# Strassen products for the second MoE matmul of three experts, in an attention + MoE kernel on one Trainium2 core

## The chip, the core and the metric

The kernel runs on one core of one Trainium2 chip. The engines named below are TensorE (PE; its weight loads are shown as PEld), VectorE (DVE), ScalarE (ACT), GpSimd (POOL) and SyncE (SP), which here only issues DMAs. The metric is the device time in microseconds. An execution taken by the profiler is described by its span (first to last instruction) and by its own time, which is a little longer.

## The reference

```python
kv  = einsum('bhsd,bhse->bhde', k, v); out = einsum('bhsd,bhde->bhse', q, kv)
x   = out / sqrt(mean(out*out, -1) + 1e-6) * g_norm         # 2304 tokens x 512
p   = domain_probs / (domain_probs.sum(-1) + 1e-9)          # 4 experts
for e in range(4):
    h = maximum(x @ w1[e], 0)                               # first product, 512 -> 1024
    y += p[:, e:e+1] * (h @ w2[e])                          # second product, 1024 -> 512
# soft MoE on y: logits = y @ phi, softmax over tokens (dispatch) and over slots (combine),
# 8 experts x 4 slots, each maximum(slot @ w1, 0) @ w2, then combine @ slot_out
```

## The kernel before

The 2304 tokens are 18 tiles of 128, in five chunks: chunks 0 to 3 of four tiles, chunk 4 of two. Chunks 0 and 1 form the first group, 2 to 4 the second. In the first group the experts run in the order 0, 1, 2, 3, in the second in the order 3, 2, 1, 0, so that expert 3's weights stay. For each expert and chunk there is a first product (called (1, c) here, function `mm1`) and a second product ((2, c), `mm2`). Every factor is split into two f16 parts, high and low, and a product is three matmuls (high high, high low, low high).

The first product is a Strassen product with seven block products in place of eight: the sums of blocks of x are made once per chunk, those of w1 per expert (`PrepW1`, on POOL), each then split by ACT (line 567) and DVE (line 569). `mm1` is called for each product P in `ORDER` and for each half u of the outputs: 14 steps of 12 matmuls, with 256 columns for a four-tile chunk and 128 for chunk 4 (line 702). Several products add up in one PSUM bank, and between them an engine reads the bank: ACT copies it (line 720), DVE adds it to an earlier copy (lines 723, 728), ACT writes relu's high part (line 711) and DVE the low part (line 712). The next product on that bank waits for such a reading. There are two buffers of each kind of bank, one for each u.

The second product (`mm2`) is a plain one: for each tile of 128 tokens 24 matmuls of 512 columns (line 760) add up in one bank, and DVE adds it, times p, to the sum over the experts (line 771, line 769 for the first expert).

The program's order is written out by hand. A list `main` holds the steps of PE. Work for the other engines is put between them: `chain` spreads a list of small steps (weight preparation, attention of a later chunk, dispatch) over a stretch of `main`, with a weight of 0.55 for steps of a first product. Each engine runs its instructions in the order in which they were written. SBUF is handed out as 47 pages of 512 KB (`Page`); loads go through one SP queue in a fixed order (`loads`, `pump`, line 152) as pages come free, at most nine held until the last expert. In the second group the weights of experts 2, 1, 0 are read again and prepared again (`prep_w1`, `prep_w2`).

After the last expert, the soft MoE's weights (`m1`, `m2a`, `m2b`, 32 MB) are read through the same queue and used.

## Time and profile before

| | before |
|---|---|
| median of 3 runs | 864.11 us (863.99 to 864.43) |
| profiled execution, own time | 864.39 us |
| its span | 862.6 us |
| PE busy | 832.7 us, 97% of the span |
| DVE, ACT, POOL busy | 472.3, 344.1, 91.1 us |
| instructions | 15472 |
| DMA | 82.89 MB, mean 96 GB/s |

In the profile, the busy time of PE holds matmuls that overlap; the mean duration of one matmul is longer than the distance to the next. In the chain of waits a stretch names the instructions that followed each other without a wait. "Idle before" is the time an engine stood still before an instruction, with what ended it.

### The profile page before, as it was taken

Reading aid. Unit: us, or ns where it says so; the run is one execution under the profiler, and the core shown is the slowest. Engines: PE = TensorE matmul, PEld = TensorE weight load, DVE = VectorE, ACT = ScalarE, POOL = GpSimd, SP = SyncE. Lnnn points to the kernel's source line nnn. Section 1 sums busy time; section 2 is a strip of 40 time slices with the busy share of each in tenths; the row PEclk is TensorE's granted clock in tenths of the full one; section 3 lists DMA queues with packets and bytes.
Section 4 is the critical chain, followed back from the end, with each engine's and each line's share of the span. In section 5 each row is a group of like instructions: output and inputs, shape, how many; then the busy total and the mean of one; then the engine's idle time right before and its main releaser. Section 6 shows DMA issues by size and latency. Waiting matters only on the chain.

```text
span 862.6 us, 15472 instructions
## 1 busy us (share of the span) xinstructions
PE 832.7 (97%) x6621; PEld 562.8 (65%) x6621; DVE 472.3 (55%) x867; ACT 344.1 (40%) x659; POOL 91.1 (11%) x57
## 2 busy tenths in 40 slices
PE   8789899999999999999999999999999999999995
PEld 7675748576666767658485685766675684864444
DVE  3788888647765344535858753536434542342314
ACT  2675563453355133515454442513423330431213
POOL 2204611201120000000211202002110000000000
PEclk8899999999999999999999999999999999999998
DMA  8720410230050400320001400140000550166687
GB/s 335 304 74 1 149 47 1 61 136 1 2 185 17 141 2 25 98 74 1 1 2 49 171 2 1 49 145 4 1 25 25 196 195 1 67 248 224 220 343 221
DMA packets 29190, 82.89 MB, mean 96 GB/s; under 512 B 3009, under 2 KB 10049, under 8 KB 29121
## 3 DMA queue, kind: packets, MB, share of 16 engines
q1 hardware_dynamic: 28672, 81.80, 26.7%
q8 instruction: 52, 0.85, 0.4%
q10 hardware_dynamic: 448, 0.10, 0.1%
q14 instruction: 18, 0.14, 0.0%
HBM read 77.17 MB, written 4.72 MB: 95 GB/s over the span
## 4 chain that ended last, share of the span: by engine, by line
PE 84%; ACT 1%; DVE 1%; issue 0%; DVEq 0%; ACTq 0%
PE y L760 40%; PE p L702 34%; PE s L1305 2%; PE so L1343 2%; PE o L301 1%; PE x2T L788 1%; PE lg L811 1%; PE kv L246 1%; PE sp L882 1%; PE xT L370 1%; ACT t L720 0%; PE f L1393 0%; ACT pages L567 0%; DVE pages L388 0%; DVE t L728 0%
## 5 line engine op out<-in xcount | busy, mean ns | idle before, releaser
L760 PE MATMUL y<-pages 128*128 128x512 f16 x1728 | 381.7, 379 | 0.0
L702 PE MATMUL p<-pages 128*128 128x256 f16 (+1 forms) x3360 | 344.3, 263 | 9.7 <-ACT t L720 6.2
L702 PEld LDWEIGHTS <-pages 128*128 128x128 f16 x3360 | 301.3, 98 | 49.2 <-issue 12.7
L760 PEld LDWEIGHTS <-pages 128*128 128x128 f16 x1728 | 168.4, 98 | 194.9 <-issue 2.9
L720 ACT COPY t<-p 128x512 f32<-128x512 f32 (+1 forms) x120 | 64.3, 538 | 219.1 <-PE p L702 219.0
L569 DVE SCALAR_TENSOR_TENSOR pages<-pages,s_w 128x512 f16<-128x512 f32 x154 | 122.0, 827 | 5.0 <-ACT pages L567 5.0
L601 POOL TENSOR_TENSOR pages<-pages 128x1024 f32<-128x1024 f32 x28 | 70.8, 2530 | 506.8 <-DVE pages L569 176.7
L567 ACT ACTIVATE pages<-pages,s_w 128x512 f16<-128x512 f32 x154 | 101.7, 711 | 44.4 <-POOL pages L601 18.2
L711 ACT ACTIVATE pages<-t 128x512 f16<-128x512 f32 (+1 forms) x120 | 70.3, 587 | 99.3 <-DVE t L723 69.9
L771 DVE SCALAR_TENSOR_TENSOR pages<-y,pc,pages 128x512 f32<-128x512 f32 x54 | 40.5, 750 | 125.0 <-PE y L760 125.0
L712 DVE SCALAR_TENSOR_TENSOR pages<-t,pages 128x512 f16<-128x512 f32 (+1 forms) x120 | 85.1, 711 | 6.3 <-ACT pages L711 1.8
L723 DVE TENSOR_TENSOR t<-p,t 128x512 f32<-128x512 f32 (+1 forms) x80 | 50.7, 634 | 64.0 <-PE p L702 62.5
L728 DVE TENSOR_TENSOR t<-p,t 128x512 f32<-128x512 f32 (+1 forms) x40 | 25.5, 638 | 70.3 <-ACT t L720 70.3
L712 DVE SCALAR_TENSOR_TENSOR pages<-p,pages 128x512 f16<-128x512 f32 (+1 forms) x40 | 25.2, 630 | 2.5 <-ACT pages L711 2.4
L438 ACT CAST pages<-pages 128x512 f16<-128x512 f32 (+1 forms) x36 | 19.2, 564 | 9.9 <-POOL pages L388 4.1
L1314 POOL MEMSET pages<- 128x1024 f32 x2 | 1.8, 952 | 184.1 <-PE s L1305 184.1
L711 ACT ACTIVATE pages<-p 128x512 f16<-128x512 f32 (+1 forms) x40 | 20.7, 542 | 1.4 <-PE p L702 1.4
L301 PE MATMUL o<-kvs,pages 128*128 128x128 f32 (+1 forms) x160 | 21.0, 296 | 0.0
L301 PEld LDWEIGHTS o<-kvs,pages 128*128 128x128 f32 (+1 forms) x160 | 19.7, 200 | 1.4 <-issue 0.2
L769 DVE TENSOR_SCALAR pages<-y,pc 128x512 f32<-128x512 f32 x18 | 13.4, 747 | 12.2 <-PE y L760 12.2
L499 DVE TENSOR_REDUCE mx_w<-pages 128x1 f32<-128x1024 f32 x16 | 18.9, 1208 | 0.0
L440 DVE TENSOR_TENSOR pages<-pages 128x512 f16<-128x512 f32 (+1 forms) x26 | 16.5, 659 | 3.4 <-ACT pages L438 3.4
(166 smaller groups left out, 405.1 us busy)
## 6 DMA issues: line engine op xcount, KB each, us to landing
pages<-in_w SPq DMA_DIRECT2D x56, 512.0 KB, 4.9
pages<-in_m SPq DMA_DIRECT2D x32, 512.0 KB, 6.1
pages<-in_m2a SPq DMA_DIRECT2D x16, 512.0 KB, 4.1
pages<-in_m2b SPq DMA_DIRECT2D x16, 512.0 KB, 10.1
pages<-in_qT SPq DMA_DIRECT2D x9, 512.0 KB, 7.1
out<-pages SPq DMA_DIRECT2D x17, 256.0 KB, 2.9
pages<-in_k SPq DMA_DIRECT2D x8, 512.0 KB, 5.7
pages<-in_v SPq DMA_DIRECT2D x8, 512.0 KB, 6.4
```

The lines of the kernel that those rows point to most:

```text
L301: nc.tensor.matmul(ps[a:z, hp * 128:hp * 128 + 128], qp[:, hp, o + a:o + z], kvbd[b % 2][:, hp, :], start=True, stop=True,)
L567: nc.scalar.activation(dst[:, 0], src, AF.Copy, scale=s)
L569: nc.vector.scalar_tensor_tensor(out=dst[:, 1], in0=src, scalar=s, in1=dst[:, 0], op0=ALU.mult, op1=ALU.subtract)
L601: self.eng.tensor_tensor(out=self.src(op).ap, in0=a.ap, in1=b.ap, op=ALU.subtract)
L702: nc.tensor.matmul(ps[:, fp * n:fp * n + n], l, r, start=(fp + i == 0 and P in (1, 2, 7)), stop=(fp == 1 and i == len(mms) - 1 and P in (2 ...
L711: nc.scalar.activation(hh, src, AF.Relu)
L712: late.append(lambda: nc.vector.scalar_tensor_tensor(out=hl, in0=src, scalar=0.0, in1=hh, op0=ALU.max, op1=ALU.subtract))
L720: nc.scalar.copy(t, ps)
L723: nc.vector.tensor_tensor(out=t, in0=ps, in1=t, op=ALU.add)
L728: nc.vector.tensor_tensor(out=d[5], in0=d["z"], in1=d[5], op=ALU.add)
L760: nc.tensor.matmul(ps, a, b, start=(u + kk + fp + i == 0), stop=(u == 1 and kk == 1 and fp == 1 and i == 2))
L771: nc.vector.scalar_tensor_tensor(out=x, in0=ps, scalar=pc, in1=x, op0=ALU.mult, op1=ALU.add)
```

## The change

In the second group, for experts 2, 1 and 0, the second product is a Strassen product too (`mm2_fast`), except for chunk 3 of expert 0. Seven products of h blocks and w2 blocks replace eight; a step is 12 matmuls of 256 columns, with two steps a product for a four-tile chunk and one for chunk 4. So a four-tile unit has 168 matmuls of 256 columns where there were 96 of 512, chunk 4 has 84 where there were 48. For it the outputs of the first product are needed as seven operands, each with a high and a low part (`fast_h`): ACT and DVE form them, partly from a queue `todo` from which every step of `mm1` takes two entries and every step of `mm2_fast` one (`work_off`). The order of `mm1`'s products becomes `ORDER2`. The order of the chunks becomes `FASTSEQ`: the second product of a chunk runs after the first product of the next. Outputs leave PSUM as 128x256 additions on DVE, seven for two tiles.

The weight operands are no longer prepared in the second group. The split operands of w1 and w2 of experts 0 to 2 are written to DRAM in the first group (`lay_aside`), together with four sums of w2 blocks, for which w2 is read a second time (`want_t`, `prep_t2`: eight POOL subtractions, eight splits on ACT and DVE per expert). In the second group 15 pages per expert are read back. The w1 scale goes from 8 to 4.

```diff
-W1S = 8.0
+W1S = 4.0
...
+ORDER2 = (1, 2, 6, 7, 5, 4, 3)
+ORDER3 = (1, 7, 6, 4, 5, 2, 3)
...
-    LASTSEQ = [(1, 2), (2, 2), (1, 3), (1, 4), (2, 4), (2, 3)]
+    KEPT = E - 1
+    FAST = list(range(E - 1))
+    FASTSEQ = [(1, 2), (1, 3), (2, 2), (1, 4), (2, 3), (2, 4)]
+    LASTSEQ = [(1, 2), (1, 4), (2, 2), (1, 3), (2, 4), (2, 3)]
...
+            key = loads[0][0]
+            if key[0] in ("o1", "o2") and now < gate[key[1]]:
+                return
...
+    def want_t(e):
+        for b in range(4):
+            want(("w2", 1, e, b), w2[e, b], 2)
     for e in range(1, E):
-        want_w(0, e)
+        for b in range(4):
+            want(("w1", 0, e, b), w1[e, b], 2)
+        if e > 1:
+            want_t(e - 2)
...
+    want_t(E - 2)
...
+    def lay_aside(e, key, pg):
+        d = aside[key[0], e, key[1]] = dram.tile([128, 2, 512], F32, name=f"{key[0]}_{e}_{key[1]}", tag=f"{key[0]}_{e}_{key[1]}")
+        nc.sync.dma_start(out=d, in_=pg.f32(2))
+    def want_back(e):
+        for key in [("o1", o) for o in (B11, B21, T2, T3, T1, T4, B22)] + [
+                ("o2", b) for b in (0, 1, "t0", "t1", "t2", "t3", 2, 3)]:
+            loads.append(((key[0], e, key[1]), lambda k=(key[0], e, key[1]): aside[k], 2))
     for e in range(E - 2, -1, -1):
-        want_w(1, e)
+        want_back(e)
...
+    def prep_t2(e, eng):
+        st = []
+        def make(j, op):
+            p, q = (need(("w2", 1, e, b)).f32(2) for b in (j, 2 + j))
+            left, right = slice(0, 256), slice(256, 512)
+            o, a, b = {
+                T1: lambda: (p[:, :, left], p[:, :, right], p[:, :, left]),
+                T3: lambda: (p[:, :, right], q[:, :, right], p[:, :, right]),
+                T2: lambda: (q[:, :, right], q[:, :, right], p[:, :, left]),
+                T4: lambda: (q[:, :, left], q[:, :, left], q[:, :, right]),
+            }[op]()
...
+            eng.tensor_tensor(out=o, in0=a, in1=b, op=ALU.subtract)
...
+        def away(b):
+            pg = w2p[1, e].pop(f"t{b}")
+            lay_aside(e, ("o2", f"t{b}"), pg)
+            pg.release()
+        for j in range(2):
+            st += [lambda j=j, op=op: make(j, op) for op in (T1, T3, T2, T4)]
+            bi = [(b, i) for b in (j, 2 + j) for i in range(2)]
+            st += stagger([lambda b=b, i=i: w2_split(e, b, f"t{b}", i, 0) for b, i in bi],
+                          [lambda b=b, i=i: w2_split(e, b, f"t{b}", i, 1) for b, i in bi])
+            st += [lambda: None, lambda: None] + [lambda b=b: away(b) for b in (j, 2 + j)]
...
+    def work_off(n, c=None, op=None):
+        while todo and (n > 0 or any(o == (c, op) for o, _ in todo)):
+            todo.popleft()[1]()
+            n -= 1
...
+        def hi(v, op, src, relu):
+            dst = hop(wk, c, op, v)[:, 0]
+            if relu:
+                nc.scalar.activation(dst, sh(src), AF.Relu)
+            else:
+                nc.scalar.copy(dst, sh(src))
+        def lo(v, op, src, relu):
+            h = hop(wk, c, op, v)
+            if relu:
+                nc.vector.scalar_tensor_tensor(
+                    out=h[:, 1], in0=sh(src), scalar=0.0, in1=h[:, 0], op0=ALU.max, op1=ALU.subtract
+                )
+            else:
+                nc.vector.tensor_tensor(out=h[:, 1], in0=sh(src), in1=h[:, 0], op=ALU.subtract)
+        def comb(v, op, out, a, op1):
+            nc.vector.scalar_tensor_tensor(out=out, in0=a, scalar=0.0, in1=out, op0=ALU.max, op1=op1)
+            hi(v, op, out, False)
+        def then(op, f):
+            todo.append(((c, op), f))
+        t1 = ht1[c, 0], ht1[c, 1]
+        t6, t7, t4 = ([hraw(wk, c, op, v) for v in range(2)] for op in (S4, S1, A12))
+        if P == 1:
+            nc.scalar.copy(t1[u], ps)
+        elif P == 6:
+            nc.scalar.copy(t6[u], ps)
+        elif P == 7:
+            nc.scalar.copy(t7[u], ps)
+        elif P == 2:
+            nc.vector.tensor_tensor(out=t1[u], in0=ps, in1=t1[u], op=ALU.add)
+            hi(u, A11, t1[u], True)
+            then(A11, lambda: lo(u, A11, t1[u], True))
+        elif P == 5:
+            nc.vector.tensor_tensor(out=t7[u], in0=ps, in1=t7[u], op=ALU.add)
+            hi(u, A22, t7[u], True)
+            then(A22, lambda: lo(u, A22, t7[u], True))
+        elif P == 4:
+            nc.scalar.activation(t4[u], ps, AF.Relu)
+            def s3():
+                nc.vector.scalar_tensor_tensor(out=t1[u], in0=t1[u], scalar=0.0, in1=t4[u], op0=ALU.max, op1=ALU.subtract)
+                hi(u, S3, t1[u], False)
+            then(S3, s3)
+            if u == 1:
+                for v in range(2):
+                    then(S3, lambda v=v: lo(v, S3, t1[v], False))
+                for v in range(2):
+                    then(S2, lambda v=v: comb(v, S2, t1[v], t7[v], ALU.subtract))
+                for v in range(2):
+                    then(S1, lambda v=v: comb(v, S1, t4[v], t7[v], ALU.add))
+                for v in range(2):
+                    then(S2, lambda v=v: lo(v, S2, t1[v], False))
+                for v in range(2):
+                    then(S1, lambda v=v: lo(v, S1, t4[v], False))
+        else:
+            nc.vector.tensor_tensor(out=t6[u], in0=ps, in1=t6[u], op=ALU.add)
+            if u == 1:
+                then(A12, lambda: [hi(v, A12, t6[v], True) for v in range(2)])
+                for v in range(2):
+                    then(A12, lambda v=v: lo(v, A12, t6[v], True))
+                for v in range(2):
+                    then(S4, lambda v=v: comb(v, S4, t1[v], t6[v], ALU.subtract))
+                for v in range(2):
+                    then(S4, lambda v=v: lo(v, S4, t1[v], False))
...
+            b = {1: "x", 6: "x", 7: "x", 4: "x", 2: "y", 5: "z", 3: "z"}[P]
+            first, end = (1, 2, 5), (2, 3, 4)
...
+            fast_h(wk, c, u, P, d, ps)
+            work_off(2)
...
+    MM2 = {1: (A11, 0, 0, 0), 2: (A12, 1, 0, 0), 3: (S4, 1, 1, 0), 4: (A22, 1, 0, 1), 5: (S1, 0, 0, 1),
+           6: (S2, 1, 1, 1), 7: (S3, 0, 1, 1)}
...
+    def mm2_fast(wk, c, P, j):
+        op, row, side, made = MM2[P]
+        work_off(1, c, op)
+        nh = len(CH[c]) // 2
+        b = {1: "x", 6: "x", 5: "x", 3: "x", 2: "y", 7: "z", 4: "z"}[P]
+        if j == 0 and P in (1, 2, 7):
+            mbank[b] = (ps_yz if P == 2 else ps_o)(f"m{P}_{wk[0]}_{wk[1]}_{c}")
+        ps = mbank[b][:, 256 * j:256 * j + 256]
+        mms = []
+        for kb in range(4):
+            h = hop(wk, c, op, kb // 2)[:, :, kb % 2]
+            key = 2 * row + kb // 2
+            w = w2_page(wk, f"t{key}" if made else key).f16().rearrange("p (s k n) -> p s k n", s=2, k=2)[:, :, kb % 2]
+            hh, hl = (h[:, s, 128 * j:128 * j + 128] for s in range(2))
+            wh, wl = (w[:, s, 256 * side:256 * side + 256] for s in range(2))
+            mms += [(hh, wh), (hh, wl), (hl, wh)]
+        for i, (l, r) in enumerate(mms):
+            nc.tensor.matmul(
+                ps, l, r, start=(i == 0 and j == 0 and P in (1, 2, 7)),
+                stop=(i == len(mms) - 1 and j == nh - 1 and P in (2, 3, 4)), skip_group_check=True,
+            )
+        if j < nh - 1:
+            return
+        half, lo = {1: (0, 0), 2: (0, 0), 7: (1, 256), 6: (1, 0), 4: (1, 0), 5: (1, 256), 3: (0, 256)}[P]
+        for i in range(nh):
+            t = CH[c][half * nh + i]
+            x = acc_f32(t)[:, lo:lo + 256]
+            nc.vector.scalar_tensor_tensor(
+                out=x, in0=mbank[b][:, 256 * i:256 * i + 256], scalar=pcs[wk[1]][:, t:t + 1], in1=x, op0=ALU.mult, op1=ALU.add
...
+            if gi == 1 and e in FAST:
+                seq = LASTSEQ if last else FASTSEQ
             for n, (which, c) in enumerate(seq):
+                fast = gi == 1 and e in FAST and not (last and c == DISP[-1])
...
+                elif fast:
+                    st = [lambda wk=wk, c=c, P=P, j=j: mm2_fast(wk, c, P, j)
+                          for P in ORDER3 for j in range(len(ch) // 2)]
...
-    for e in range(E - 2, -1, -1):
-        chain(m["mm1", 1, e + 1, 3 if e == E - 2 else 2], m["end", 1, e + 1, 4] - 1, prep_w1(1, e, P) + prep_w2(1, e), 12)
+    for e in FAST:
+        if e < E - 2:
+            chain(m["mm1", 0, e + 1, 0] + 2, m["mm1", 0, e + 1, 1], prep_t2(e, P), 4)
+        else:
+            chain(m["mm1", 0, e + 1, 1], m["end", 0, e + 1, 1], prep_t2(e, P), 4)
+        gate[e] = m["mm1", 1, e + 1, 3]
+    for e in range(E - 1):
+        for i, op in enumerate((B11, B21, T2, T3, T1, T4, B22)):
+            hooks.setdefault(m["mm1", 0, e, 1] + 1 + i, []).append(
+                lambda e=e, op=op: lay_aside(e, ("o1", op), wop[0, e][op]))
+        for b in range(4):
+            hooks.setdefault(m["mm2", 0, e, 1] + 1 + b, []).append(
+                lambda e=e, b=b: lay_aside(e, ("o2", b), w2p[0, e][b]))
+    hooks.setdefault(m["mm1", 1, E - 2, 2], []).append(
+        lambda: hsets.extend([Page() for _ in range(7)] for _ in range(2)))
+    hooks.setdefault(m["mm1", 1, 0, 4], []).append(lambda: [hsets[1].pop().release() for _ in range(3)])
     lastc = DISP[-1]
-    chain(m["end", 1, 0, 2], m["mm1end", 1, 0, 4], disp_steps(2), 0, 1.0)
+    chain(m["end", 1, 0, 2], m["end", 1, 0, 4], disp_steps(2), 0, 1.0)
```

## Rows read from the trace of the kernel before

**Rows 1.** The page: busy time of PE, and the chain that ended last by engine.

```profile
PE 832.7 (97%) x6621; PEld 562.8 (65%) x6621; DVE 472.3 (55%) x867; ACT 344.1 (40%) x659; POOL 91.1 (11%) x57
...
PE 84%; ACT 1%; DVE 1%; issue 0%; DVEq 0%; ACTq 0%
```

**Rows 2.** Chain in order of time, expert 2, second group: start us, us, what.

```profile
496.74 18.42 PE p L702 x168
515.15 20.72 PE y L760 x96
...
575.01 6.04 PE p L702 x108
...
582.66 2.17 PE p L702 x36
584.84 10.36 PE y L760 x48
595.20 4.91 PE p L702 x45
```

**Rows 3.** Timeline of ACT in (1, 1) of expert 1, products 5 and 3.

```profile
181.28 0.59 ACT L720 COPY t<-p 128x512 f32<-128x512 f32 x1 [1.06 <-PE p L702]
182.62 0.63 ACT L711 ACTIVATE pages<-t 128x512 f16<-128x512 f32 x1 [0.76 <-DVE t L728]
183.16 0.57 ACT L720 COPY t<-p 128x512 f32<-128x512 f32 x1
```

**Rows 4.** Timeline of DVE and PE in the same unit.

```profile
169.29 18.58 PE L702 MATMUL p<-pages 128*128 128x256 f16 x168
...
170.16 1.41 DVE L569 SCALAR_TENSOR_TENSOR pages<-pages,s_w 128x512 f16<-128x512 f32 x2
...
181.90 0.69 DVE L728 TENSOR_TENSOR t<-p,t 128x512 f32<-128x512 f32 x1 [4.54 <-ACT t L720]
```

**Rows 5.** Groups by line and shape: line, engine, names, shapes, count | busy us, mean ns | idle before.

```profile
L712 DVE SCALAR_TENSOR_TENSOR pages<-t,pages 128x512 f16<-128x512 f32 x96 | 71.6, 747 | 4.2 <-ACT pages L711 0.4
L723 DVE TENSOR_TENSOR t<-p,t 128x512 f32<-128x512 f32 x64 | 44.1, 688 | 60.6 <-PE p L702 60.5
L723 DVE TENSOR_TENSOR t<-p,t 128x256 f32<-128x256 f32 x16 | 6.6, 419 | 3.4 <-PE p L702 2.1 <-ACT t L720 1.3
L711 ACT ACTIVATE pages<-t 128x512 f16<-128x512 f32 x96 | 60.5, 630 | 90.5 <-DVE t L723 65.1 <-DVE t L728 25.2
L440 POOL TENSOR_TENSOR pages<-pages 128x512 f16<-128x512 f32 x6 | 7.2, 1232 | 0.0
```

**Rows 6.** Timeline of (1, 1) of expert 0, where ACT waits for POOL.

```profile
97.76 3.49 DVE L569 SCALAR_TENSOR_TENSOR pages<-pages,s_w 128x512 f16<-128x512 f32 x2
97.92 2.79 POOL L601 TENSOR_TENSOR pages<-pages 128x1024 f32<-128x1024 f32 x1 [2.56 <-DVE pages L569]
...
100.74 1.33 ACT L567 ACTIVATE pages<-pages,s_w 128x512 f16<-128x512 f32 x2 [3.16 <-POOL pages L601]
...
102.59 1.47 PE L702 MATMUL p<-pages 128*128 128x256 f16 x12 [1.42 <-ACT t L720]
```

**Rows 7.** Windows: from:to us, PE, PEld, DVE, ACT, POOL busy, PEclk, DMA share, GB/s.

```profile
148.50:169.40 20.90, 20.90 (x101) 9.71 (x99) 14.27 (x23) 9.02 (x15) 5.54 (x2) 1.00 0.09 26
169.40:187.90 18.50, 18.50 (x170) 16.42 (x168) 9.22 (x14) 11.47 (x21) 0.00 (x0) 1.00 0.57 199
751.00:766.30 15.30, 14.32 (x212) 12.77 (x210) 11.14 (x33) 8.49 (x24) 0.00 (x0) 1.00 0.54 199
816.00:822.00 6.00, 6.00 (x59) 2.01 (x56) 0.65 (x3) 0.96 (x2) 0.00 (x0) 1.00 1.02 406
```

**Rows 8.** The clock after a stop of PE: a timeline row and a window.

```profile
56.70 2.33 PE L702 MATMUL p<-pages 128*128 128x256 f16 x12 [2.31 <-ACT t L720]
...
58.00:62.00 4.00, 4.00 (x27) 3.61 (x26) 3.15 (x5) 3.32 (x7) 0.00 (x0) 0.68 0.02 4
```

More of the change, by code (lines that the diff above doesn't have):

```diff
@@ L648, in prep_w1, with w2_split @@
         return st + [lambda n=n: step(n) for n in range(len(seq) + 1)]
+    def w2_split(e, b, key, i, part):
+        pgs = w2p.setdefault((0 if key == b else 1, e), {})
+        if key not in pgs:
+            pgs[key] = Page(True)
+        dst = pgs[key].f16().rearrange("p (s k n) -> p s k n", s=2, k=2)
+        src = ("w2", 0 if key == b else 1, e, b)
+        split(dst[:, :, i], need(src).f32(2)[:, i], wpw[e, "w2"][1], part)
+        if i == 1 and part == 1:
+            drop(src)
+    def prep_t2(e, eng):
[20 more added lines that the diff above has]
+            st += [lambda: None, lambda: None] + [lambda b=b: away(b) for b in (j, 2 + j)]
+        return st
     def prep_w2(g_, e):
@@ L657, in sp @@
         def sp(b, i, part):
-            pgs = w2p.setdefault((g_, e), {})
-            if b not in pgs:
-                pgs[b] = Page(True)
-            dst = pgs[b].f16().rearrange("p (s k n) -> p s k n", s=2, k=2)
-            split(dst[:, :, i], raw(b).f32(2)[:, i], wpw[e, "w2"][1], part)
-            if i == 1 and part == 1:
-                drop(("w2", g_, e, b))
+            w2_split(e, b, b, i, part)
         bi = [(b, i) for b in (0, 2, 1, 3) for i in range(2)]
@@ L680, in attn_moe_softmoe_kernel, with w1_page, w2_page, hset @@
     us = [{}, {}]
-    def mm1(wk, c, u, P):
+    def w1_page(wk, op):
+        pgs = wop.setdefault(wk, {})
+        if op not in pgs:
+            pgs[op] = need(("o1", wk[1], op))
+        return pgs[op]
+    def w2_page(wk, b):
+        pgs = w2p.setdefault(wk, {})
+        if b not in pgs:
+            pgs[b] = need(("o2", wk[1], b))
+        return pgs[b]
+    hsets = []
+    todo = deque()
+    def hset(wk, c):
+        return hsets[c == (4 if wk[1] == 0 else 3)]
+    def hraw(wk, c, op, u):
+        pgs = hset(wk, c)
+        if len(CH[c]) == 2:
+            i = 2 * SLOT[op] + u
+            return pgs[i // 4].f32(4)[:, i % 4]
+        return pgs[SLOT[op]].f32(2)[:, u]
@@ L702, in mm1 @@
                 nc.tensor.matmul(
-                    ps[:, fp * n:fp * n + n], l, r, start=(fp + i == 0 and P in (1, 2, 7)), stop=(fp == 1 and i == len(mms) - 1 and P in (2, 3, 4)),
+                    ps[:, fp * n:fp * n + n], l, r, start=(fp + i == 0 and P in first), stop=(fp == 1 and i == len(mms) - 1 and P in end),
                         skip_group_check=True,
                 )
+        if fast:
+            if P == 1:
+                ht1[c, u] = w512(f"t1_{nm}")[:, :2 * n]
+                ht1.setdefault((c, 1 - u), None)
+            fast_h(wk, c, u, P, d, ps)
+            work_off(2)
+            return
         def put(src, kk, half):
@@ L983, in start_chunk @@
     def start_chunk(c):
-        hbuf[c] = [Page() for _ in range(len(CH[c]))]
+        hbuf[c] = [Page() for _ in range(len(CH[c]))] if hbuf.get(c) is None else hbuf[c]
     def end_chunk(c):
@@ L1208, in attn_moe_softmoe_kernel @@
                 h()
[L1209 removed]
+            idle[0] = None if i >= m["mm2", 1, 0, lastc] else lend[i]
             run_bg(i)
```

82 lines of the change are left out of this document (58 added, 24 removed).

## The prediction

> **What bounds the kernel now.** I read the page first: PE is busy for 97% of the span and the chain that ended last is PE for 84% [rows 1]. So what counts is the work on PE, and each wait that stops it. Next I read the chain over one expert of the second group [rows 2]. A four-tile first product takes 18.42 us for 168 matmuls of 256 columns (0.1096 each), a four-tile second product 20.72 us for 96 of 512, the second product of chunk 4 10.36 us; each starts where the one before ends. Only chunk 4's first product has a gap: its first 9 steps take 6.04 us, 0.671 a step, so 14 would be 9.40, and from 575.01 to 584.84 it takes 9.83. The whole expert takes 595.20 - 496.74 = 98.46 us. Then I read how an engine clears a bank between two products [rows 3, 4]. Product 5 of the unit that starts at 169.45 ends after nine steps of 1.316, at 181.29. ACT copies at 181.28 (0.59), DVE adds at 181.90 (0.69), ACT writes relu's high part at 182.62 (0.63), and only then, in ACT's order, comes the copy for the other half, 183.16 to 183.73. Product 3 of that half is due at 169.45 + 11 x 1.316 = 183.93. So one round ACT, DVE, ACT leaves 0.2 us. Throughput is not short, but the turn-around is.
>
> **The columns saved.** A `mm2_fast` step has the shape of a first product's step. A four-tile unit costs 168 x 0.1096 = 18.42 us instead of 20.72, chunk 4 9.21 instead of 10.36 [rows 2]. Five four-tile units and three of chunk 4 are changed: 5 x 2.30 + 3 x 1.15 = 14.95 us off PE's path. This is the whole gain; prep removed from DVE, ACT and POOL in the second group was beside PE and gives nothing by itself.
>
> **The operands of h, walked in order.** Prices: a DVE operation on 128x512 gives its result after 0.75, an addition from PSUM after 0.69, ACT's high part after 0.63 [rows 5]. On one engine the next starts about 0.08 earlier than that: two of 0.75 take 1.41 [rows 4], ACT's follow 0.54 apart [rows 3]. So 0.67, 0.61 and 0.54 when queued; a handover 0.03 to 0.05. A four-tile unit asks DVE for 6 additions, 14 low parts, 8 combinations and 14 output additions of 128x256 (0.42 [rows 5], 0.36 queued): 3.7 + 14.7 + 5.0 = 23.4 us in PE's 36.8. On average there is room. The order is the trouble.
>
> Within (1, 2), count from the end of product 5 for u = 0. DVE adds (0.69), ACT writes the high part (0.63), and as `work_off` takes the low part in the same step, DVE stands waiting for ACT and then writes it (0.75): 2.15 us with handovers, where PE's step is 1.32. The second half begins at 2.15 and ends at 4.3. Then the difference S3 of u = 0 (to 5.0); the relu of product 4 for u = 1 is in ACT's queue behind S3's high part, so it is ready at 6.2 and S3 of u = 1 at 6.95; then one low part, addition, low part, combination, addition, two combinations: to 11.5. PE's last step ended at 5 x 1.316 = 6.58. So DVE is 4.9 us late at the end of every four-tile first product, and 12 entries of `todo` remain.
>
> (1, 3) follows at once. From its start: ACT's first copy waits behind the high part of the last combination and is ready at 6.2; product 6 was due at 4 x 1.316 = 5.26: PE stops 1.0. DVE ends four more entries at 7.6, the addition of product 2 at 8.2, another entry 8.9, the second addition 9.6. ACT, with two high parts of A12 put before it, writes the second high part at 10.6 and only then copies product 6: 11.2. Product 7 was due at 7.9 + 1.1: 2.1 lost. Its other half waits for a copy behind two combinations: another 0.95. A restart costs 0.16 (36 matmuls take 2.17 where 3 x 0.671 = 2.01 [rows 2]), so 4.5 us in all. From product 5 on the unit is as (1, 2), and again leaves DVE 4.9 late. In (2, 2) the output additions of product 1 stand behind two entries: ready at 7.1, product 6 due at 5.26: 2.0 lost. By the same walk with 0.42 for small operations [rows 5], (1, 4) loses 0.7, (1, 2) itself 0.3. Between (2, 3) and (2, 4) the first bank comes free only after product 3's two output additions, which begin when PE ends: 1.1. Together 0.3 + 4.5 + 2.0 + 0.7 + 1.1 = 8.6 us, against 5.75 saved and the 0.43 that (1, 4) lost before [rows 2]: +2.4 us for expert 2 and +2.4 for expert 1.
>
> Expert 0 has (1, 4) right behind (1, 2): the same 12 large entries meet steps of 0.671. The copy of product 6 is ready at about 10.1 where product 7 is due at 4.0; the stops come at products 2, 6 and 7, 6.3 by then with restarts, and the other half of product 7 adds 2.0: 8.3. With 0.3 in (1, 2) and 3.45 saved (one 2.30, one 1.15), and without the 0.98 of PE idle that this expert had in its old (1, 4) [rows 7], +4.2. Second group: 2.4 + 2.4 + 4.2 = +9.0 us.
>
> **The first group.** Per expert 8 POOL subtractions of 128x512 (1.23 each [rows 5]), 8 ACT and 8 DVE splits are added. They start no later than two steps into a unit. In the three first products that they cross, one ACT split (0.6) falls between the high part and the copy of product 5, where 0.2 us was left: 0.4 + 0.16, about 1.7 for three. In the second product that follows, DVE is busy 14.27 of 20.9 us [rows 7]; six low parts add 4.0. A make on POOL can hold up DVE: while one of 2.79 ran, two DVE splits took 3.49 instead of 1.41 [rows 6]. Five makes add 0 to 6.2, so DVE ends up to 3.5 us late; the next unit leaves it 9 of 18.5 us free [rows 7]. ACT waiting for POOL did stop PE by 1.42 in such a place [rows 6]. I take 0 to 3.5 for each of two experts (expert 2's makes run where POOL has no other weights). Bounds 0 and 1.7 + 7 = 8.7; I take 3, nearer to the unit that has room.
>
> The Trainium skill, SBUF — State Buffer, section "SBUF: two separate sides", says that DVE with two SBUF inputs and a GpSimd operation that reads SBUF exclude each other for the whole instruction. By that rule every make that meets a split costs its whole length, the upper bound above; the trace shows one split in two extended.
>
> **Queues, pages, scale.** Each expert adds 15 writes and 15 reads of 512 KB on SP and 4 reads of w2, and takes 8 reads out. At 406 GB/s [rows 7] a page takes 1.3 us: 15 take 19, inside an expert of about 95. A write waits on SP for a split that is already done; behind it stand the next expert's loads, a few us, with a unit of 18 us before their use. Writes hold their pages until they land; I price this with the 0 to 8.7. The last w2 pages of an expert are read while (1, 2) and the next unit run, 27 us in the shortest case. The soft MoE's loads start later, since h takes 14 pages; of their 64 pages 47 fit, 61 us at that rate, and about 90 us remain after the last (1, 2): 0, at most 3. The scale and the product order change no count: 0.
>
> **Sum.** 864.39 + 9.0 + 3 = 876.4 for an execution as the profiled one, which was 0.28 above the median: 876.1 us.
>
> **Rivals.**
> *The queues keep up.* If neither of the lags at the ends of first products reaches PE, because `todo` is worked off before it matters, the columns stand: 14.95 less the two waits between (2, 3) and (2, 4) (2.2) and 0 to 3 of the first group gives about 852. For it: DVE has 23.4 us of work in 36.8. Against: the order in ACT's queue, and a trace in which a single round is as tight as a step. 0.18.
> *The clock falls.* After a stop of 2.31 us the granted clock was 0.68 over 4 us [rows 8], at the lower of its levels (1.2 GHz) for 2.6 of them: 1.3 lost. After 1.42 it did not fall. If it falls in both (1, 3) and twice in the last (1, 4): +5, 881. 0.10.
> *The first group saturates DVE*, as with the lock above: +8.7 instead of 3, 882; decided where DVE's lag passes the 5.2 us (20.72 / 4) that a second product's spare bank gives it. 0.08.
> *The read-back is late.* If SP stands more than 17 us behind (27 less 8 pages of 1.3), PE waits at (2, 2): some 6 us, 882. No load here is that late. 0.04.
>
> **How the numbers follow.** The forecast has 0.60. About 0.2% is what a measurement can tell from no change: 862.4 to 865.8. The stops are differences of long sums: with every DVE and ACT price 10% lower the walk gives 97.0 for an expert in place of 100.9 and 2.2 less for expert 0, and without a first-group cost 863.4; 0.06 of the 0.60 lies within the bound. Upward, prices 5% higher give 2.3 more for each expert and 1.4 for expert 0, and 8.7 for the first group: 888. Faster 0.18, same 0.06, slower 0.54 + 0.22 = 0.76. The range 860 to 887 leaves out most of the first rival and little above.
>
> **What would show it.** Four-tile `mm2_fast` without stops: 18.4 us. Expert 2's chain: (1, 3) of about 23 us, with stops before products 6 and 7 released by ACT's copy; (2, 2) of 20.4, with a stop before product 6 released by DVE; the last (1, 4) about 17.7. In the first group stops below 1 us at product 3 of three units. If (1, 3) takes under 19 us, the walk is wrong and the first rival holds; idle before loads would show the fourth, a clock below 1 in the second group the second.

## The result and the profile after

The changed kernel takes 870.95 us (median; 870.41 to 871.56) against 864.25 us for the kernel before: a ratio of 1.0078, 95% interval 1.0061 to 1.0095. So it is slower by 6.7 us, where 12 were forecast. The profiled execution of the kernel after took 870.41 us with a span of 868.6, that of before 864.39 with 862.6: 6.0 us to be found.

The page of the kernel after, its busy time and the chain by engine (answering [rows 1]):

```profile
PE 821.4 (95%) x7089; PEld 609.2 (70%) x7089; DVE 523.8 (60%) x1002; ACT 350.6 (40%) x681; POOL 96.0 (11%) x69
...
PE 68%; DVE 12%; ACT 6%; issue 1%; DMA 0%; SPq 0%; DVEq 0%; ACTq 0%
```

The busy time of PE fell by 11.3 us and the span grew by 6.0; the chain, which was PE for 84%, is now PE for 68%, DVE for 12% and ACT for 6%. Work was taken off PE and waits were put in. The bytes written to DRAM rose from 4.72 to 28.31 MB, those read from 77.17 to 94.47. No share of the chain is DMA, so the rival with the late read-back is out at this point.

The places where PE stopped in the kernel after, from its timeline: start, duration, what ran then, how long PE had stood before it and what ended that. First the first group; none of these five is in the trace of before.

```profile
120.64 1.46 PE L955 MATMUL y<-pages 128*128 128x512 f16 x6 [2.00 <-DVE pages L964]
146.31 4.09 PE L890 MATMUL p<-pages 128*128 128x256 f16 x36 [0.53 <-ACT t L915]
180.02 10.88 PE L890 MATMUL p<-pages 128*128 128x256 f16 x96 [0.81 <-DVE t L918]
226.82 4.09 PE L890 MATMUL p<-pages 128*128 128x256 f16 x36 [0.58 <-ACT t L915]
260.51 10.88 PE L890 MATMUL p<-pages 128*128 128x256 f16 x96 [0.80 <-DVE t L918]
```

Then the second group: the first five rows are expert 2 (expert 1 has the same five, 97.3 us later), the last five expert 0.

```profile
523.50 2.78 PE L890 MATMUL p<-pages 128*128 128x256 f16 x24 [0.31 <-ACT t L819]
528.01 1.47 PE L890 MATMUL p<-pages 128*128 128x256 f16 x12 [1.73 <-ACT pages L821]
530.22 9.33 PE L890 MATMUL p<-pages 128*128 128x256 f16 x84 [0.75 <-ACT pages L821]
545.90 13.26 PE L991 MATMUL m<-pages 128*128 128x256 f16 x120 [1.11 <-DVE pages L1001]
563.71 5.52 PE L890 MATMUL p<-pages 128*128 128x128 f16 x96 [0.53 <-ACT pages L821]
...
715.77 0.83 PE L890 MATMUL p<-pages 128*128 128x128 f16 x12 [0.97 <-DVE pages L853]
717.95 1.62 PE L890 MATMUL p<-pages 128*128 128x128 f16 x24 [1.35 <-ACT t L819]
721.77 0.83 PE L890 MATMUL p<-pages 128*128 128x128 f16 x12 [2.19 <-ACT pages L821]
724.20 6.20 PE L890 MATMUL p<-pages 128*128 128x128 f16 x84 [1.60 <-ACT pages L821]
769.29 0.33 PE L1090 MATMUL dtr<-ident,dT 128*128 128x128 f32 x1 [1.73 <-ACT dT L1082]
```

Line 819 is ACT's copy of product 1 (PE waits to go on to product 6), line 821 that of product 6 (the step after is product 7), line 1001 an output addition of `mm2_fast`: the places and releasers that the prediction named. Expert 2's chain in [rows 2] had one gap; here it has five.

The 6.0 us by parts, from where each expert starts in the two traces. Expert 3 of the second group keeps its weights and follows on the first group without a gap:

| part | before | after | difference | forecast |
|---|---|---|---|---|
| first group, to expert 3's start in it | to 287.57 | to 292.48 | +4.9 | +3 |
| expert 3, both groups | to 496.74 | to 499.40 | -2.25 | 0 |
| expert 2 | 98.46 | 97.34 | -1.1 | +2.4 |
| expert 1 | 98.51 | 97.33 | -1.2 | +2.4 |
| expert 0, to the start of the tail | 112.5 | 118.2 | +5.7 | +4.2 |
| tail | 56.4 | 56.3 | 0 | 0 |

The first row holds a difference that is not of the change. At the stop of 1.4 us that both kernels have in (1, 1) of expert 0, before any of the five, the kernel after was ahead by 0.87 (101.72 against 102.59), and a kernel below that differs from it in the second group alone (the second form of fewer entries) reached that place at 102.53. From there on the first group lost 5.8, of which the five stops are 4.72 and a restart of 0.16 after each 0.8.

### The profile page after: what moved, and what is told of

It is laid out like the page before. It is cut to its first block, busy times and chain, and to the rows that moved or that the text cites. A ratio compares the mean times of both kernels' runs of the same rounds, so it can differ in the third digit from the quotient of the medians.

```text
span 868.6 us, 16718 instructions
## 1 busy us (share of the span) xinstructions
PE 821.4 (95%) x7089; PEld 609.2 (70%) x7089; DVE 523.8 (60%) x1002; ACT 350.6 (40%) x681; POOL 96.0 (11%) x69
## 3 DMA queue, kind: packets, MB, share of 16 engines
HBM read 94.47 MB, written 28.31 MB: 141 GB/s over the span
## 4 chain that ended last, share of the span: by engine, by line
PE 68%; DVE 12%; ACT 6%; issue 1%; DMA 0%; SPq 0%; DVEq 0%; ACTq 0%
PE y L955 24%; PE p L890 22%; PE m L991 13%; DVE pages L603 2%; PE s L1578 2%; DVE pages L802 2%; ACT pages L795 1%; PE so L1616 1%; DVE pages L806 1%; PE o L335 1%; ACT t L915 1%; PE x2T L1020 1%; DVE t L810 1%; DVE t L825 1%; PE lg L1043 1%
## 5 line engine op out<-in xcount | busy, mean ns | idle before, releaser
L890 PEld LDWEIGHTS <-pages 128*128 128x128 f16 x3360 | 302.5, 98 | 63.2 <-issue 29.2
L955 PE MATMUL y<-pages 128*128 128x512 f16 x1104 | 246.1, 379 | 2.5 <-DVE pages L964 2.0
L955 PEld LDWEIGHTS <-pages 128*128 128x128 f16 x1104 | 107.3, 98 | 125.8 <-issue 5.8
L991 PE MATMUL m<-pages 128*128 128x256 f16 x1092 | 121.0, 273 | 2.2 <-DVE pages L1001 2.2
L991 PEld LDWEIGHTS <-pages 128*128 128x128 f16 x1092 | 106.6, 98 | 15.8 <-issue 3.4
L601 ACT ACTIVATE pages<-pages,s_w 128x512 f16<-128x512 f32 x112 | 73.5, 711 | 37.8 <-POOL pages L635 12.0
L906 ACT ACTIVATE pages<-t 128x512 f16<-128x512 f32 (+1 forms) x72 | 44.0, 612 | 71.5 <-DVE t L918 53.2
L1001 DVE SCALAR_TENSOR_TENSOR pages<-m,pc,pages 128x256 f32<-128x256 f32 x91 | 40.8, 481 | 40.7 <-PE m L991 40.6
L907 DVE SCALAR_TENSOR_TENSOR pages<-t,pages 128x512 f16<-128x512 f32 (+1 forms) x72 | 54.6, 761 | 3.0 <-ACT pages L906 0.6
L918 DVE TENSOR_TENSOR t<-p,t 128x512 f32<-128x512 f32 (+1 forms) x48 | 31.7, 664 | 35.2 <-PE p L890 35.2
L635 POOL TENSOR_TENSOR pages<-pages 128x1024 f32<-128x1024 f32 x16 | 40.3, 2521 | 96.6 <-DVE pages L603 62.8
L707 POOL TENSOR_TENSOR pages<-pages 128x512 f32<-128x512 f32 x24 | 35.6, 1484 | 81.2 <-DMA pages<-in_w 78.8
L923 DVE TENSOR_TENSOR t<-p,t 128x512 f32<-128x512 f32 (+1 forms) x24 | 16.1, 669 | 30.7 <-ACT t L915 30.6
## 6 DMA issues: line engine op xcount, KB each, us to landing
pages<-in_m2b SPq DMA_DIRECT2D x16, 512.0 KB, 10.1
```

What stands on the lines that cost most here:

```text
L601: nc.scalar.activation(dst[:, 0], src, AF.Copy, scale=s)
L635: self.eng.tensor_tensor(out=self.src(op).ap, in0=a.ap, in1=b.ap, op=ALU.subtract)
L707: eng.tensor_tensor(out=o, in0=a, in1=b, op=ALU.subtract)
L890: nc.tensor.matmul(ps[:, fp * n:fp * n + n], l, r, start=(fp + i == 0 and P in first), stop=(fp == 1 and i == len(mms) - 1 and P in end), ...
L906: nc.scalar.activation(hh, src, AF.Relu)
L907: late.append(lambda: nc.vector.scalar_tensor_tensor(out=hl, in0=src, scalar=0.0, in1=hh, op0=ALU.max, op1=ALU.subtract))
```

## The experiments

The theory after the result: the places are right, the second group loses its gain to entries of `todo` that stand in DVE's and ACT's queues ahead of the readings of banks; the first group loses to the sums of w2; and expert 3 gains since the preparation of weights has left its stretch. The rivals: the loss of the second group is DVE's quantity of work, not its order; the first group's loss is the DMA writes; and its stop of 2.00 us is the order of the splits on DVE, not POOL.

**One entry at a time.**

```diff
             fast_h(wk, c, u, P, d, ps)
-            work_off(2)
+            work_off(1)
...
-        work_off(1, c, op)
+        work_off(1 if wk[1] else 2, c, op)
```

> Each step of a first product takes one entry of todo instead of two (in expert 0 each step of the second product takes two instead of one, so that the queue is empty before chunk 3). Theory (the stops of PE come from ACT's copies queued behind parts that wait for DVE): DVE is at most 2.5 us late where it was 4.9, (1, 3) takes 18.4 us where it took 21.7, (2, 2) 18.4, the last (1, 4) about 12 where it took 17.9, with the granted clock at 1.00 there; an expert takes 93.7 where it took 97.3; together about 858 us, between 856 and 862. Rival (the loss comes from the added DMA traffic or from narrower matmuls): the rate at which entries are taken changes nothing, 871.

It took 858.4 us (856.99 to 859.84), ratio 0.9929 [0.9912, 0.9947]. Its chain over expert 2, in order of time:

```profile
506.80 18.50 PE p L890 x168
...
525.32 10.64 PE p L890 x96
535.96 18.35 PE m L991 x168
...
559.57 5.52 PE p L890 x96
565.09 27.51 PE m L991 x252
```

(1, 3) and (2, 2) run without a stop. Why can be read on DVE in (1, 3). In the kernel after, the addition of line 825 (product 2 of the first half) stands behind a row of entries of the list, among them these:

```profile
521.57 1.29 DVE L810 SCALAR_TENSOR_TENSOR pages<-pages 128x512 f32<-128x512 f32 x2
522.77 1.29 DVE L806 TENSOR_TENSOR pages<-t,pages 128x512 f16<-128x512 f32 x2
523.97 0.69 DVE L806 TENSOR_TENSOR pages<-pages 128x512 f16<-128x512 f32 x1
524.57 0.69 DVE L825 TENSOR_TENSOR t<-p,t 128x512 f32<-128x512 f32 x1
```

With one entry a step, DVE reaches the same addition early and waits for PE, not PE for it:

```profile
519.86 1.29 DVE L810 SCALAR_TENSOR_TENSOR t<-pages,t 128x512 f32<-128x512 f32 x2
521.48 0.69 DVE L825 TENSOR_TENSOR t<-p,t 128x512 f32<-128x512 f32 x1 [0.33 <-PE p L890]
```

The start of (1, 3) is 0.5 us earlier in this kernel, the addition 3.1. Both kernels have the same operations. So it is the order, not the quantity: experts 2 and 1 take 93.71 us each, 3.6 less than after, and only (1, 4) still stops there, by 1.25. The last (1, 4), of expert 0, has 2.31 of stops (0.62 and 1.69) where the kernel after has 6.11.

**The parts of a step after the list.**

```diff
+            work_off(2)
             fast_h(wk, c, u, P, d, ps)
-            work_off(2)
```

> Each step takes its two entries of todo before the new outputs are read and not after, so a low part comes one step after its high part; all else as after. Theory (DVE falls behind within a first product because it waits for ACT's high part in the same step): DVE is 3.0 us late at its end and not 4.2, the stop of 1.1 in (2, 2) of experts 2 and 1 goes, the stops in (1, 3) and in the last (1, 4) stay, since the same entries stand before product 6: 868.6 us. Rival (the lateness is the sum of DVE's work): 871.

869.81 us (868.67 to 871.7), ratio 1.0063 [1.0049, 1.0077]. The stop in (2, 2) is gone, those in (1, 3) and in the last (1, 4) stay; in the chain:

```profile
532.46 9.33 PE p L890 x84
541.79 18.40 PE m L991 x168
```

An expert takes 96.13 us (597.77 - 501.64), 1.2 less than after. The two gains are 2.4; against the kernel before beside it the kernel is slower by 5.0 where the kernel after was slower by 6.7, so 1.7 of them show. In the profiled execution, the slowest of the four, the 84 matmuls of the last (1, 4) took 7.69 us instead of 6.20, at a granted clock of 0.50 from 724 to 728. For an expert, the order within one step does a third of what the number of entries taken per step does.

**Without the sums.**

```diff
-            want_t(e - 2)
...
-            chain(m["mm1", 0, e + 1, 0] + 2, m["mm1", 0, e + 1, 1], prep_t2(e, P), 4)
```

(both readings and both calls are left out)

> Left out: the four sums of w2 blocks per expert, with the second reading of w2, the subtractions, the splits and their 12 writes; the Strassen products use the plain w2 operands in their place, read back twice. Theory (the first group's loss of 4.9 us is the preparation of these sums): first group as before, 866 us. Rival (writing the operands to DRAM costs it): 33 of 45 writes are left, so at most a quarter of it goes, 869.7 or more.

865.99 us (865.69 to 866.62), ratio 1.002 [1.0011, 1.0029], as expected. All five stops of the first group are gone while 22.02 of the 28.31 MB are still written, so it is the sums, with what is read and written for them, and not the writes of the other operands. Expert 2 starts at 494.50, 2.2 us earlier than in the kernel before.

**Only the reading back, with a plain second product.**

```diff
-    FAST = list(range(E - 1))
+    FAST = []
```

(with the old orders of chunks and dispatch, and without the sums)

> One part alone: the operands of w1 and w2 are written to DRAM in the first group and read back in the second, with no sums and no preparation there; the second product is the plain one everywhere, in the order of before. Theory (preparation in the second group held up PE: 2.25 us in expert 3, 0.3 to 0.4 in each (1, 4)): 861.3 us, between 860.5 and 862.5. Rival (preparation there was hidden beside PE, as predicted): 864.2. Rival (the DMA traffic costs): above 865.

862.76 us (862.16 to 863.16), ratio 0.998 [0.9971, 0.9989]. The time is 0.3 above the range expected. Expert 2 starts at 494.02, 2.7 us earlier than before, of which 0.5 is there when expert 3 starts in the first group (287.10) and 2.25 comes in expert 3, as in the kernel after; experts 2 and 1 take 98.63 and 98.57 as they did. So the gain is in expert 3 alone; the second part of the expectation, that (1, 4) would lose its short stop, failed: it stops by 0.29 to 0.34 all the same.

Why expert 3 gains is seen in the kernel before, in rows that I had not read ahead of the prediction. The timelines of POOL, DVE and PE in it:

```profile
416.09 4.85 POOL L601 TENSOR_TENSOR pages<-pages 128x1024 f32<-128x1024 f32 x2 [171.42 <-DVE rms L354]
...
418.76 2.46 DVE L388 TENSOR_TENSOR pages<-pages 128x256 f32<-128x256 f32 x1
...
422.55 0.66 PE L370 MATMUL xT<-ident,pages 128*128 128x128 f32 x4 [1.42 <-DVE pages L359]
```

POOL subtracts for expert 2's weights; meanwhile a sum of x blocks for a later chunk (line 388) takes DVE 2.46 us, and PE stops for 1.42 in expert 3.

**The kernel before, with these differences on DVE.**

```diff
-... prep_w1(1, e, P) + prep_w2(1, e), 12)
+... prep_w1(1, e, V if e == E - 2 else P) + prep_w2(1, e), 12)
```

> The kernel before, with the four subtractions that prepare w1 of expert 2 in the second group on DVE in place of POOL. Theory (POOL runs the first two as soon as the loads land, at 416 us, and holds up DVE's attention work there, which is the 2.2 us by which the changed kernel is quicker in expert 3 of the second group): 862.2 us, between 861.5 and 863.3. Rival (that gain comes from the splits that are no longer there, or from DMA): 864.4 or more.

863.2 us (862.37 to 863.86), ratio 0.9983 [0.9974, 0.9992]. The DVE step now takes 0.43 in its timeline:

```profile
418.46 0.43 DVE L388 TENSOR_TENSOR pages<-pages 128x256 f32<-128x256 f32 x1
```

The stop at 422 is gone and expert 2 starts at 495.55, 1.2 earlier. That is half of the 2.25; DVE now has the subtractions itself, with a new stop of 0.32 (at 449.07). The other half is a second stop of the kernel before, 0.90 in (1, 4) of expert 3, which stays here. Its chain shows what made it:

```profile
483.29 0.61 ACT pages L567
...
484.21 2.17 PE p L702 x36
```

A split of expert 2's weights on ACT (line 567) stands for 0.61 ahead of the copy for which PE waits. Without the preparation (read-back alone, without the sums, kernel after) that stop is 0.29. So of the 2.25, 1.42 and a restart were POOL's subtractions and 0.61 was the ACT split.

**The sums on DVE.**

```diff
-... prep_t2(e, P), 4)
+... prep_t2(e, V), 4)
```

(in both calls)

> The eight subtractions that make the sums of w2 blocks run on DVE instead of POOL; all else as after. Theory (POOL runs them as soon as the loads land and holds up DVE's splits): the stop of 2.0 us at the second product of (2, 1) of expert 0 is gone, 868.5 us; DVE gets 5 us more per expert, so the stops of 0.8 at the start of the next unit may stay or grow: 867.5 to 870. Rival (the added splits and not POOL cost the time): 871 or more.

871.52 us (869.74 to 872.76), ratio 1.0074 [1.0057, 1.0091]: a miss, at the time that the rival gave. The stops of 2.00 and 0.8 went, and those at product 3 grew (timeline of PE):

```profile
146.58 4.09 PE L890 MATMUL p<-pages 128*128 128x256 f16 x36 [1.87 <-ACT t L915]
...
227.62 5.76 PE L890 MATMUL p<-pages 128*128 128x256 f16 x36 [1.99 <-ACT t L915]
```

The subtractions stand in DVE's queue ahead of the addition for which ACT's high part, and with it the next copy, waits: ACT's copy of product 5 ends at 142.72, DVE subtracts from 143.51 and adds from 144.11. The second row holds a fall of the clock too: 36 matmuls take 5.76 where they took 4.09, at a granted clock of 0.58 from 228 to 232. Without POOL the wait is paid in another place; beside a first product the work cost PE time on either engine.

**The sums later, on POOL.**

```diff
-            chain(m["mm1", 0, e + 1, 0] + 2, m["mm1", 0, e + 1, 1], prep_t2(e, P), 4)
+            chain(m["mm1", 0, e + 1, 0] + 10, m["mm1", 0, e + 1, 1] + 6, prep_t2(e, P), 4)
```

> The steps that make the sums of w2 blocks start eight steps later in experts 0 and 1 (at product 3 of (1, 0) of the next expert) and run six steps longer; still on POOL. Theory (POOL has nothing else to do and runs them when the loads land, long before their place in the order): the stop of 2.0 us in (2, 1) of expert 0 stays at the same place; the stops of 0.5 to 0.6 before product 3, made by an ACT split in that place, go; the stops of 0.8 at the next unit stay or grow to 1.5: 869 to 871. Rival (POOL's subtractions run where they stand in the order): the stop of 2.0 is gone or comes 11 us later.

874.2 us (873.8 to 875.25), ratio 1.0115 [1.01, 1.0131]. The stop of 2.0 stays and those of 0.53 and 0.58 go (0.36 is left, at 188.12), as expected, but the time is 3 us above the range. POOL's timeline in it:

```profile
112.52 4.63 POOL L707 TENSOR_TENSOR pages<-pages 128x512 f32<-128x512 f32 x3 [4.82 <-DMA pages<-in_w]
...
169.14 6.74 POOL L707 TENSOR_TENSOR pages<-pages 128x512 f32<-128x512 f32 x4
```

Although their place in the program is eight steps later, the first subtractions still run at 112 us, when their pages land, and PE still stops (2.03, at 121.07). The order written out by hand orders an engine only against what it waits for; POOL has nothing before these in its queue. The second four run at 169.14, where they ran at 162.68 in the kernel after, nearer to the start of the next unit, which now stops PE by 1.97 (at 178.38) and, an expert later, by 1.96 (at 259.76), more than the 1.5 allowed for; at the latter the clock fell as well (0.57 from 260 to 264).

**The second read later.** What can hold POOL back is the load.

```diff
-        if e > 1:
+        if e > 2:
             want_t(e - 2)
         for b in range(4):
             want(("w2", 0, e, b), w2[e, b], 2)
+        if e == 2:
+            want_t(0)
```

> The kernel after with one change of order: the second read of w2 of expert 0 is put behind expert 2's first read of w2 in the queue of loads, so that POOL cannot subtract at 112 us. Theory (POOL runs a subtraction as soon as its pages have landed, however early that is before its place in the order, and holds up DVE): the three subtractions of 4.98 leave 112 us, the six DVE splits at 112.8 take about 4.1 to 5 instead of 7.1, and the PE stop of 2.00 at 120.64 falls under 0.4. They land somewhere in the next unit and may cost up to 0.8 there: 869.0 to 870.2. Rival (the stop is the work that DVE has in its order there): the stop stays near 2.0 and the time at 870.9.

869.22 us (868.93 to 869.64), ratio 1.0053 [1.0039, 1.0067]. The timelines of POOL and DVE in the kernel after:

```profile
112.41 4.98 POOL L707 TENSOR_TENSOR pages<-pages 128x512 f32<-128x512 f32 x3 [5.11 <-DMA pages<-in_w]
...
112.81 7.11 DVE L603 SCALAR_TENSOR_TENSOR pages<-pages,s_w 128x512 f16<-128x512 f32 x6
```

and with the later load:

```profile
112.09 4.06 DVE L605 SCALAR_TENSOR_TENSOR pages<-pages,s_w 128x512 f16<-128x512 f32 x6
...
130.31 1.28 POOL L709 TENSOR_TENSOR pages<-pages 128x512 f32<-128x512 f32 x1 [24.39 <-DVE pages L966]
133.63 4.30 POOL L709 TENSOR_TENSOR pages<-pages 128x512 f32<-128x512 f32 x3 [2.05 <-DMA pages<-in_w]
```

The same six splits take 4.06 us where they took 7.11, the stop of 2.00 is gone, expert 3 starts 1.8 earlier, and the other four stops stay (0.53, 0.80, 0.58, 0.80). So that stop was POOL, early; its rival, the order on DVE, falls. The Trainium skill, SBUF — State Buffer, section "SBUF: two separate sides", says that a DVE operation with two SBUF inputs and a GpSimd operation that reads SBUF exclude each other, the later one waiting until the earlier ends; the trace agrees: three subtractions of 4.98 us cost six splits 3.05. Three of the splits take 1.76, the other three 0.74; a split and a subtraction take turns, so DVE lost about 1.0 for each subtraction, not its whole 1.66.

**Fewer entries and the sums on DVE together**, and then the first alone.

```diff
-            work_off(2)
+            work_off(1)
...
-        work_off(1, c, op)
+        work_off(1 if wk[1] and j else 2, c, op)
```

(in the first of the two also the late start above, on DVE)

> One entry a step in first products, in second products two in a product's first step and one in its second (two always in expert 0); the sums of w2 blocks for experts 0 and 1 on DVE, started eight steps later, ending six steps later. Theory: as with one entry a step (858.4), with 1.0 us less in (1, 4) of experts 2 and 1, and 3 to 5.4 us less in the first group: 852 to 855. Rival (DVE has no room left in the first group's second products): 857 to 860.

859.41 us (857.94 to 861.41), ratio 0.9942 [0.9929, 0.9955]. The second group did as expected, 92.67 us an expert, with 0.21 left of the stop in (1, 4). The first group lost more than any: expert 2 starts at 505.39, with rows like these on PE:

```profile
178.64 5.40 PE L890 MATMUL p<-pages 128*128 128x256 f16 x48 [1.32 <-DVE t L918]
186.00 7.07 PE L890 MATMUL p<-pages 128*128 128x256 f16 x48 [1.96 <-ACT t L915]
```

In the second of them the clock fell too (48 matmuls in 7.07 instead of 5.40, granted 0.77 and 0.81 from 184 to 192). The rival held: late in a second product and early in the next unit DVE has no room for the subtractions.

> Two edits of the kernel after: a first product's step takes one entry from the list of parts, and in expert 1 and 2 a fast second product takes two entries only at its second step of each product. The sums stay where the kernel after has them, on POOL. This is the second-group half of e7 alone. In e7 the experts 2 and 1 took 92.67 us each where e1_one_entry had 93.71, and its first group lost 8.65 where that of the kernel after loses about 4.9 less the 2.25 of the kept expert. If the two halves of e7 do not touch each other, this kernel takes 858.4 - 2 x 1.04 = 856.3, with expert 2 at 92.7. Rival: the loss of e7 came from the changed pops; then expert 2 starts as late as in e7 (505) and the time is about 859.4.

857.27 us (855.73 to 859.55), ratio 0.9915 [0.9901, 0.9929], with 92.67 us for expert 2 and for expert 1. Against the kernel before beside each it is 1.5 us better than one entry everywhere, where 2.1 were expected. The profiled execution, the slowest of the five, lost 3.3 us to the clock in two places (below); whether the median lost to it too, no trace shows.

**Fewer entries and the later read.**

> The edits of e9_one_entry_b and e10_later_second_read together. If they add up, e9 less what e10 gains over the kernel after: about 855 with 1.3 gained, 856.3 with nothing gained. Rival: the later subtractions meet DVE in a first product and cost as in e6, 1 to 2 us: 857.5 to 858.5.

854.24 us (853.37 to 855.17), ratio 0.988 [0.9867, 0.9894]: 10.5 us faster than the kernel before (864.7 in this comparison), and the fastest kernel here. It is 3.0 below fewer entries alone, where the later read by itself gained 2.2 (each against the kernel before beside it). So the two edits add up, within the 3.8 us over which the runs of the former spread.

## Why the prediction was right, and where its size was wrong

*What counts is the stops of PE, from the order in ACT's and DVE's queues.* Right: of the stops that the walk (the step by step count of the two queues) named in the second group, those in (1, 3), (2, 2) and both kinds of (1, 4) are there, with the releasers named, and taking fewer entries a step removed those in (1, 3) and (2, 2).

*The columns.* Right: an unhindered (2, 2) takes 18.35 us for 168 matmuls where 18.42 was the price, and (2, 3) with (2, 4) 27.51 for 252.

*The size of the walk for experts 2 and 1, +2.4 each.* Wrong: -1.1 and -1.2. Part by part for expert 2, from the rows above: (1, 2) 0 lost (0.3 forecast), (1, 3) 2.79 in stops, 3.3 with restarts (4.5), (2, 2) 1.11, 1.3 with its restart (2.0), (1, 4) 0.53, 0.7 with its restart (0.7), between (2, 3) and (2, 4) 0 (1.1). Two steps failed. The first is the price of a DVE operation, 0.75, and 0.67 when it follows another; (1, 3) and (2, 2) lost 1.9 less by it. The groups by line and shape in the kernel after:

```profile
L907 DVE SCALAR_TENSOR_TENSOR pages<-t,pages 128x512 f16<-128x512 f32 x66 | 52.0, 792 | 2.5 <-ACT pages L906 0.4
L802 DVE SCALAR_TENSOR_TENSOR pages<-pages 128x512 f16<-128x512 f32 x20 | 13.4, 689 | 7.1 <-ACT pages L795 7.0
```

Both lines write low parts of relu, but line 907 runs in the first group and for expert 3, in part beside POOL. The mean of 747 ns in [rows 5] was such a mixture: between 100 and 300 us, where POOL prepares weights, that group has a mean of 839 ns, and 687 from there on. In the second group of the kernel after, where POOL is idle, one operation takes 0.69 and a following one 0.60 (two take 1.29). The 1.41 for two in [rows 4] was another operation, line 569. ACT's prices were right (0.63, and 0.52 to 0.54 apart), so the prediction's own trial with all prices 10% lower, which gave 97.0 for an expert where 97.34 was measured, is no proof; the places in (1, 2) and (1, 3) of expert 2 are. From DVE and ACT:

```profile
511.50 0.69 DVE L829 TENSOR_TENSOR pages<-p,pages 128x512 f32<-128x512 f32 x1 [4.00 <-PE p L890]
...
522.87 0.58 ACT L819 COPY t<-p 128x512 f32<-128x512 f32 x1
...
527.39 0.56 ACT L821 COPY pages<-p 128x512 f32<-128x512 f32 x1
```

From the first addition of product 5 (511.50) to the second combination at the end (the first of the two of line 810 at 521.57, which ends at 522.26) the walk had 11.5 and the trace has 10.8. (1, 3) starts at 517.82; its first copy is ready 5.6 later (6.2 in the walk) and the copy of product 6 10.1 later (11.2). So the order of the walk holds, and with DVE's smaller price each place comes earlier by 0.6 to 1.1. The second step that failed is the 1.1 between (2, 3) and (2, 4): 252 matmuls run there without a wait. Two output additions do begin when (2, 3) ends, at 587.61, and end at 588.49, but PE did not wait for the bank that they read; why not stays open.

*Expert 0, +4.2.* It was +5.7, by two terms. The last (1, 4) took 17.9 us as forecast (17.7), but by 6.1 of stops, 0.64 of restarts and 1.4 of a fallen clock (84 matmuls in 6.20, where 96 take 5.52 at the full clock, so 84 take 4.83), where the forecast had 8.3 of stops and restarts; that the two agree is luck. And the 0.98 of idle time in the old (1, 4) [rows 7] was counted as gone. It was the dispatch's wait for ACT; the dispatch moved to (1, 3) with it, and there it is 1.73 (row at 769.29; before, 0.86). A step that is moved takes its waits along. From the chains of the kernels before and after:

```profile
756.58 1.28 ACT L850
```

```profile
767.44 1.28 ACT L1082
```

Both are a table load (ACT_TABLE_LOAD in the timeline) ahead of the dispatch's exponential, and PE goes on 1.84 us after it begins in both. In the kernel before PE ran out of work 0.98 us after the load began (at 757.56), in the kernel after already 0.12 us after it (at 767.56), since in its new place the load stands behind a high part of the first product on ACT. That is the whole of the 0.87 by which the wait grew.

*First group, +3.* It was +4.9, or 5.8 without the quicker start, inside the bounds of 0 to 8.7. The two stops of 0.53 and 0.58 at product 3 came about as worked out (0.4 and a restart; two units, not three). The starts of the next units (0.81, 0.80) are the lag of DVE after a second product. The stop of 2.00 was not foreseen, since I placed the subtractions where the program has them, in the second product of a unit that starts at about 130; POOL ran the first three at 112, as soon as their pages were there.

*"Prep removed gives nothing by itself".* Wrong: -2.25, and two kernels without the change of the second product show it (read-back alone, and the kernel before with differences on DVE). POOL is busy for 11% of the span and has no share of the chain [rows 1], but its operation held DVE's, and DVE's was what PE waited for; an ACT split ahead of a copy did the rest.

*Queues, read-back, pages.* Rightly priced at nothing: no wait of PE on a load in the second group, and no difference in the tail. The rival that the queues keep up did not hold for this order of work; it did once `todo` was taken in smaller portions, and then the time went to 854 to 858, near the 852 worked out for it. The rival with the clock held in one place of the four that it named, in the profiled execution: the last (1, 4).

The two errors that lowered the time (3.5 and 3.6 for the two experts, 2.25 for expert 3: 9.35) outweigh those that raised it (1.5 for expert 0, 1.9 for the first group: 3.4): 12.0 forecast less 5.95 is 6.05, and 6.0 was measured. That the total came no further from the forecast is in part luck: the errors had both signs, and without those that raised it the difference would have been 2.7.

## What to carry to other kernels

Price a queue from operations of the stretch in question, and look at the smallest or the common duration, not at a group's mean, which takes in those held up by another engine. When work for helping engines is split into parts and taken from a list, the number taken per step can decide more than the total, as here: parts that are not yet needed must not stand in front of the reading that frees a bank. And an operation on an engine with an empty queue runs when its data land, not where the program has it; to place it, place its load.

## What the runs showed of the hardware that I had not expected

The same stops can cost a fall of the clock in one execution and none in another. The last (1, 4) with one entry per step and with its second form (timeline of PE, the former first):

```profile
711.46 5.52 PE L890 MATMUL p<-pages 128*128 128x128 f16 x96 [1.69 <-ACT pages L821]
```

```profile
712.40 7.15 PE L890 MATMUL p<-pages 128*128 128x128 f16 x96 [1.69 <-ACT pages L821]
```

Both had stood 0.62 and then 1.69; the same 96 matmuls take 5.52 or 7.15. The windows of the latter (from:to, us, busy time of PE, PEld, DVE, ACT, POOL, granted clock, DMA share, GB/s):

```profile
120.00:124.00 4.00, 2.52 (x9) 1.39 (x9) 2.55 (x7) 0.62 (x2) 0.00 (x0) 0.79 0.00 0
...
712.00:716.00 4.00, 3.60 (x38) 3.60 (x38) 1.77 (x3) 1.36 (x5) 0.00 (x0) 0.60 0.21 82
```

At 121 us this kernel's PE had stood 2.04 and the clock fell to 0.79, and 0.78 in the next 4 us (the lower level, 1.2 GHz, for part of the time); the kernel after stood 2.00 there and kept 1.00 in both windows, and in its last (1, 4) it fell to 0.62:

```profile
724.00:728.00 4.00, 3.80 (x45) 3.80 (x45) 1.76 (x5) 1.21 (x4) 0.00 (x0) 0.62 0.01 2
```

From 120.64 on the kernel after took 10.58 us to the next unit (131.22), the other 12.26 from 121.48 to 133.74. So a stop of about 2 us cost its own length in one execution and 1.7 us more in another, and its length does not tell which it will be: of five traces with that stop, those with 1.96 (the parts of a step after the list, granted 0.80) and 2.04 lost to the clock, those with 2.00, 2.00 and 2.03 did not. With it goes a wider spread of times: 3.8 us between the runs of that kernel (855.73 to 859.55), 0.9 for the kernel before beside it (864.13 to 865.01). With one entry at a time, two runs at a mean granted clock of 0.987 took 856.99 and 857.2 us, two at 0.983 859.6 and 859.84.
